# Six more groups whose skip term is turned by DMA, and two transfers moved, in a fused spectral filter and channel MLP on one core

## The chip, the core and the metric

The kernel runs on one core of one Trainium2 chip. The core's engines have queues of their own: TensorE (PE, its weight loads are listed as PEld), VectorE (DVE), ScalarE (ACT), GpSimd (POOL) and SyncE (SP), which here only issues DMAs. DMAs issued by SP and by POOL share 16 DMA engines. The metric is the device time of one execution in microseconds, less is better. Before the change three runs took 514.1, 515.17 and 517.45 us, median 515.17.

## What is computed

The input x has 8 batches of 3136 rows and 256 channels. First each channel is filtered along the rows in the frequency domain, then a low-rank mix along the rows is added, then a two-layer MLP over the channels with its skip:

```python
# x: (8, 3136, 256); filt_r, filt_i: (1569, 256)
X = np.fft.rfft(x, axis=1)
Y = X * (filt_r + 1j * filt_i)[None]
x = np.fft.irfft(Y, n=3136, axis=1)
# U: (3136, 32), V: (32, 3136), w_ch1: (256, 1024), w_ch2: (1024, 256)
xt = x.transpose(0, 2, 1)
u = x + (xt @ U @ V).transpose(0, 2, 1)
return u + np.maximum(u @ w_ch1, 0.0) @ w_ch2
```

## The kernel before

Everything is in float16 with float32 sums in PSUM. 3136 is 49 x 64, and the Fourier transforms are done as matmuls in stages. A batch goes through them in this order.

- Stage 1 (`f1`, L249; for batches 0 and 1 `f1_turned`, L282): four x tiles, loaded by POOL (`load_x`, L127), are multiplied by a 49-point transform. From batch 2 on the result goes to DRAM (`asb` to `ct1` and `ct0`, L256 and L257).
- Stages 2 and 3 (`mid`): from batch 2 on four loads bring the result back in another layout (`a` from `ct`, L327 and L330, called stage 2's loads). Thirteen items follow, each a 64-point transform (`pz`, L385), the filter on DVE (`uv`, L393, L397, L398) and the transform back (`pe`, L344, evicted by ACT at L354). The spectrum goes to DRAM (`ct2`, L363).
- `load_e2` (L417) brings the spectrum back as rows of the tile `eb`, in three parts, called the rows; `rank` adds the 32 low-rank rows.
- Stage 4 (`s4`, L457) multiplies `eb` into `ut`, which is u of one batch with the channels on the partitions.

The MLP runs on 49 groups of 512 rows, counted over all batches. For each group `mm1` (L489, ReLU on ACT at L492) makes eight hidden tiles, and `mm2` (L522) multiplies them by `w2sb`. The last loop of the kernel is the schedule, written out by hand: 392 steps, eight to a group. Step 8n + t issues `mm1(groups[n], t)`, then `mm2(groups[n - 1], t)`, then whatever `plan[8n + t]` holds. The other stages of the next batch are cut into pieces, and `deal` spreads the pieces over the plan. What a step issues on an engine stands in that order in the engine's queue, but the queues run independently of one another: SP and POOL work ahead of PE as far as data and buffers let them.

The output needs u added, and u lies transposed in `ut`. There are two ways. `residual` (L514) multiplies pieces of `ut` by an identity matrix on PE, eight matmuls for a group that lies in one batch, and DVE then copies the sum out of PSUM (L538). For the groups in `turn_at`, `turn_u` (L502) has SP issue two DMA transposes, a pair, that write the turned u into a tile `tur`, and DVE adds it while it evicts (L535). `tur` has three buffers, so each pair waits for the add of the third turned group before it. The first of a group's two evictions comes at t = 3 of its `mm2`, the second at t = 7; then POOL stores the group's output (L542).

For b from 1 to 7 the plan treats a stretch of steps from a = S[b-1] to z = S[b], in which groups of batch b-1 are mixed while batch b goes through its stages. S is 0, 48, 96, 144, 192, 240, 288, 336, 392. e is z - 17 for b = 1, z - 20 for b = 2 to 5 and z - 22 for b = 6 and 7. In a stretch, in the plan of before:

- the rows of batch b are loaded at e - 5, e - 4 and e + 1;
- stage 2's loads of batch b + 1 are issued at e + 2 (z - 12 for b = 1);
- the x loads of batch b + 1 stand at a - 8, a - 6, a - 4 and a - 2 (9, 11, 13, 15 for b = 1);
- for b > 1 three groups, a/8 + 1 to a/8 + 3, are turned at a + 1, a + 2 and a + 3, and the last whole group, z/8 - 1, at z - 9. For b = 1 these are groups 2, 3 and 4 at 15, 16 and 17, and group 5 at 39. From step 337 on groups 43 to 48 are turned in their own steps.

So groups 0, 1, 6, 10, 12, 16, 18, 22, 24, 28, 30, 34, 36, 40 and 42 go through `residual`. Ahead of the loop POOL issues the second batch's x, `w2sb` (L604) and, since nothing holds it, the third batch's first x loads.

Of the kernel before, what the change touches and what calls it, by code (L numbers as in the profile page):

```python
# [14 lines left out]
NB = 8  # L15
# [7 lines left out]
NG = NB * SEQ // GT  # L23
# [56 lines left out]
def kernel(  # L80
# [11 lines left out]
    nc = tc.nc  # L92
# [18 lines left out]
    def bank(tag, name, dtype=F32):  # L111

        return ps.tile([128, 512 if dtype == F32 else 1024], dtype, tag=tag, bufs=4 if tag == "z" else 2, name=name)

    def dram(t, off, dims):
        return bass.AP(tensor=t, offset=off, ap=[list(d) for d in dims])
# [7 lines left out]
    def load_x(b, c):  # L124
        t = sb.tile([98, 8 * DM], F16, tag="x", bufs=4, name="x")
        for a, n in ((0, 96), (96, 2)) if b == 0 else ((0, 98),):
            nc.gpsimd.dma_start(t[a:a + n], dram(x.tensor, (b * SEQ + 8 * c + 32 * a) * DM, [[32 * DM, n], [1, 8 * DM]]))  # L127
        xt[b, c] = t
# [51 lines left out]
    w2sb = cst.tile([128, 8, DM], F16)  # L180
# [16 lines left out]
    seen = cst.tile([128, 4], F16)  # L197
# [42 lines left out]
    def f1(b):  # L240
        for c in range(4):
            t = xt[b, c].rearrange("p (j d) -> p j d", d=DM)
            asb = sb.tile([98, 8, DM], F16, tag="asb", bufs=3, name="asb")
            for half in range(2):
                for i in range(2):
                    pf = bank("z", "pf")
                    for s in range(2):
                        j = 4 * half + 2 * i + s
                        nc.tensor.matmul(pf[0:98, 256 * s:256 * s + 256],  # L249
                                         ws[:, (8 * c + j) * 98:(8 * c + j + 1) * 98], t[:, j, :],  # L250
                                         start=(s == 0), stop=True, skip_group_check=True)
                    dst = asb[:, 4 * half + 2 * i:4 * half + 2 * i + 2, :]
                    src = pf[0:98].rearrange("p (j d) -> p j d", d=DM)
                    nc.scalar.copy(dst, src)  # L254
                    if half and i:
                        nc.sync.dma_start(dram(ct1[b], 8 * c * 96 * DM, [[DM, 96], [96 * DM, 8], [1, DM]]), asb[0:96])  # L256
                        nc.sync.dma_start(dram(ct0[b], 8 * c * DM, [[32 * DM, 2], [1, 8 * DM]]),  # L257
                                          asb[96:98].rearrange("p j d -> p (j d)"))
                    yield
# [8 lines left out]
    def f1_turned(b):  # L268
        t1[b] = (sb.tile([128, 2, 24, 128], F16, tag="ut", bufs=2, name="t1"),
                 sb.tile([128, 2, NR], F16, tag="t10", bufs=1, name="t10"))  # L270
        for c in range(4):
            t = xt[b, c].rearrange("p (j d) -> p j d", d=DM)
            for n in range(4):
                half, dh = n // 2, n % 2
                pf = bank("z" if b else ("z", "m", "z", "o")[n], "pf")
                if b == 0:

                    unread(pf, 2 if (c, n) == (3, 0) else 0)
                    unread(pf, 1, 120)
                for s in range(4):  # L280
                    j = 4 * half + s
                    nc.tensor.matmul(pf[:, 98 * s:98 * s + 98], t[:, j, 128 * dh:128 * dh + 128],  # L282
                                     ws[:, (8 * c + j) * 98:(8 * c + j + 1) * 98],
                                     start=(s == 0), stop=True, skip_group_check=True)
                j = 8 * c + 4 * half

                copy = nc.vector.tensor_copy if dh and not (b and c < 1) else nc.scalar.copy
                copy(t1[b][0][:, dh, :, 4 * j:4 * j + 16].rearrange("p k (j c) -> p k j c", c=4),
                     view(pf, 0, [[1, 24], [98, 4], [24, 4]]))
                copy(view(t1[b][1], NR * dh + j, [[1, 4], [32, 2]]), view(pf, 96, [[98, 4], [1, 2]]))  # L290
                yield
# [201 lines left out]
        gr.h.append(h)  # L493


    turn_at = {}

    def turn_u(gr):
        gr.tu = sb.tile([128, 2, 4, 128], F16, tag="tur", bufs=3, name="tur")
# [5 lines left out]
    def residual(gr, o, i):  # L505
        last = []
        for b, t0, so, n in gr.seg:
            a, z = max(so, 128 * i), min(so + n, 128 * i + 128)
            for dh in range(2):
                if a < z:  # L510
                    p = a - 128 * i
                    last.append((o[p:p + z - a, 128 * dh:128 * dh + 128], utv(b)[:, dh, t0 + a - so:t0 + z - so], dh))
        for d, w, dh in last:
            nc.tensor.matmul(d, w, idn, start=False, stop=(dh == 1), skip_group_check=True)  # L514

    def mm2(gr, t):
        i, half = t // 2, t % 2
        if t % 4 == 0:
            gr.pc = bank("o", "pc")
        o = gr.pc[:, 256 * (i % 2):256 * (i % 2) + 256]  # L520
        for tt in range(4 * half, 4 * half + 4):
            nc.tensor.matmul(o, gr.h[tt][:, 128 * i:128 * i + 128], w2sb[:, tt, :],  # L522
                             start=(tt == 0), stop=(tt == 7 and gr.n in turn_at), skip_group_check=True)
        if half and not gr.n in turn_at:
            residual(gr, o, i)

        parts = {3: (0, 1), 5: (2,), 7: (3,)} if gr.n == NG - 1 else {3: (0, 1), 7: (2, 3)}
        if t not in parts:
            return
        if t == 3:  # L530
            gr.och = sb.tile([128, 4, DM], F32, tag="och", bufs=2, name="och")
        a, n = parts[t][0], len(parts[t])
        dst, src = gr.och[:, a:a + n, :], gr.pc[:, 256 * (a % 2):256 * (a % 2 + n)]
        if gr.n in turn_at:
            nc.vector.tensor_add(dst.rearrange("p g (h d) -> p g h d", h=2), src.rearrange("p (g h d) -> p g h d", h=2, d=128),  # L535
                                 gr.tu[:, :, a:a + n, :].rearrange("p h g d -> p g h d"))
        else:
            nc.vector.tensor_copy(dst, src.rearrange("p (j d) -> p j d", d=DM))  # L538
        if gr.n == NG - 1:
            nc.sync.dma_start(dram(out.tensor, (gr.n * GT + 128 * a) * DM, [[DM, 128], [128 * DM, n], [1, DM]]), dst)  # L540
        elif t == 7:
            nc.gpsimd.dma_start(dram(out.tensor, gr.n * GT * DM, [[DM, 128], [128 * DM, 4], [1, DM]]), gr.och)  # L542


    S = [8 * (b * SEQ // GT) for b in range(NB)] + [8 * NG]
    plan = [[] for _ in range(8 * NG)]

    def deal(gen, count, a, z):
        for i in range(count):
            plan[max(0, int(a + i * (z - a) / count))].append(gen)  # L550

    def later_x(b, c):
        load_x(b, c)
        yield

    f1s = [f1(b) if b > 1 else f1_turned(b) for b in range(NB)]
    mids = [mid(0, "o")] + [mid(b) for b in range(1, NB)]
# [2 lines left out]
    turns = [turn_u(gr) for gr in groups]  # L560
# [38 lines left out]
    for h in range(2):  # L599
        for p in (32, 64):  # L600
            nc.gpsimd.tensor_copy(seen[p:p + 32], eb[p:p + 32, 8 + 32 * h, 0:4])  # L601
        for c in ((1,), (2, 3))[h]:
            load_x(1, c)
    nc.gpsimd.dma_start(w2sb, moe_w_ch2.rearrange("(t cc) e -> cc t e", t=8))  # L604
    for _ in s4s[0]:
        pass

    def loads(b, part):
        load_e2(b, part)
        yield  # L610

    for b in range(1, NB):
        a, z = S[b - 1], S[b]
        e = z - (17 if b == 1 else 20 if b < 6 else 22)
        deal(mids[b], 13, a + {1: 8, 2: -3}.get(b, -5), e - 4)
        deal(mids[b], 4, e - 4, e)
        for p, at in enumerate((e - 5, e - 4, e + 1)):
            plan[at].append(loads(b, p))
        deal(ranks[b], 6, e, e + 6)
        if b + 1 < NB:  # L620

            plan[z - 12 if b == 1 else e + 2].append(mids[b + 1])

        n = a // 8 + (1 if b > 1 else 2)
        turn_at.update({n + i: a + (1 if b > 1 else 15) + i for i in range(3)})
        turn_at[z // 8 - 1] = z - 9
        deal(s4s[b], 16, e + 8, z - 2)
        if b == 1:
            deal(f1s[1], 12, 1, 8)
        if b + 1 < NB:  # L630

            for c in range(4):
                plan[a + (9 if b == 1 else -8) + 2 * c].append(later_x(b + 1, c))
            deal(f1s[b + 1], 16, a + (21 if b == 1 else 10), z - (13 if b == 1 else 20))

    turn_at.update({n: 8 * n + 2 for n in range(S[NB - 1] // 8 + 1, NG)})
    for n, at in turn_at.items():
        plan[at].append(turns[n])
    for n, gr in enumerate(groups):
        for t in range(8):  # L640
            mm1(gr, t)
            if n:
                mm2(groups[n - 1], t)
            for gen in plan[8 * n + t]:
                next(gen, None)
# [32 lines left out]
```

## Time and profile before

| what | value |
|---|---|
| profiled execution, device time | 515.22 us |
| its span, first to last instruction | 513.4 us |
| mean granted TensorE clock | 0.988 |
| ACT, ReLU of `mm1` (L492) | 392 x 604 ns |
| PE, `mm2` (L522) | 1568, 234.3 us busy |
| PE, `mm1` (L489) | 896, 234.0 us busy |
| PE, identity matmuls (L514) | 128, 8 of them for pieces at a border of batches |
| DVE, add and evict (L535) / copy (L538) | 69 / 30 |
| SP, DMA transposes (L502) | 68, 1.19 to 8.83 us each to issue, median 1.33 |
| POOL, x loads of 392 KB | 28, median 10.7 us to landing |
| DMA queues, share of 16 engines | SP's 44.3%, POOL's 30.8% |

The profile is one execution; its time around the span is 1.8 us. Busy PE is modelled and matmuls overlap, so the price of a matmul is read from the distance between two starts. For DMAs issued by SP the profile tells the time of issue but not of landing; a landing shows only where something waits for it. "Idle before" in brackets names what ended an engine's idle time.

### The profile page before, as it was taken

What the parts mean: (1) busy time and instruction counts of PE and PEld (TensorE: products, weight loads), DVE (VectorE), ACT (ScalarE), POOL (GpSimd) and SP (SyncE); (2) the same over time, 40 slices, a digit from 0 to 9 for tenths busy, and PEclk for the clock granted to TensorE, in tenths of its full rate; (3) what the DMA queues carried; (4) which work ended last, traced back from release to release, by engine and by line L of the source; (5) the groups of instructions that cost most, each with busy time, mean ns of one, the idle gap of its engine ahead of it and who ended that gap; (6) DMA issues with size and microseconds to landing.
All of it is one profiled execution on the core that took longest, in us unless ns stands there. A gap on an engine that the chain in (4) does not pass through costs nothing.

```text
span 513.4 us, 11535 instructions
## 1 busy us (share of the span) xinstructions
PE 483.8 (94%) x4580; PEld 340.7 (66%) x4580; DVE 350.9 (68%) x470; ACT 375.7 (73%) x704; POOL 80.6 (16%) x122
## 2 busy tenths in 40 slices
PE   4886799996899999999999999999999999999996
PEld 4545466774576777677667777677667766776665
DVE  5886499584875797479867898479847896731122
ACT  6873678964697679866897689867996677666663
POOL 6662010020010210030010200120001010101110
PEclk9997999999899999999999999999999999999999
DMA  8987929999458996799568994899688456343243
GB/s 194 167 202 176 176 53 210 291 249 185 123 171 269 260 182 206 232 263 210 166 183 279 243 198 149 254 265 186 214 256 237 126 125 226 104 124 104 72 113 124
DMA packets 104383, 97.13 MB, mean 189 GB/s; under 512 B 41843, under 2 KB 88883, under 8 KB 104328
## 3 DMA queue, kind: packets, MB, share of 16 engines
q1 hardware_dynamic: 89624, 54.80, 44.3%
q0 software_dynamic: 14704, 41.58, 30.8%
q8 instruction: 36, 0.59, 0.4%
q14 instruction: 19, 0.16, 0.1%
HBM read 55.20 MB, written 47.78 MB: 201 GB/s over the span
## 4 chain that ended last, share of the span: by engine, by line
PE 78%; DMA 9%; DVE 6%; ACT 2%; SPq 1%; issue 1%; POOL 0%; POOLq 0%; DVEq 0%; ACTq 0%
PE pc L522 30%; PE phh L489 29%; PE pu L457 4%; PE pf L249 4%; PE pe L344 4%; DVE uv L393 3%; PE pz L385 3%; DMA tur<-ut 3%; DMA w2sb<-in_moe_w_ch_dram 2%; DMA ct<-e 2%; DMA eb<-ct 1%; PE pc L514 1%; PE ph L424 1%; ACT e L354 1%; DVE uv L398 1%; DVE uv L397 1%
## 5 line engine op out<-in xcount | busy, mean ns | idle before, releaser
L492 ACT ACTIVATE h<-phh 128x512 f16<-128x512 f32 x392 | 235.8, 604 | 81.4 <-PE phh L489 80.4
L522 PE MATMUL pc<-w2sb,h 128*128 128x256 f16 x1568 | 234.3, 273 | 2.6 <-DMA w2sb<-in_moe_w_ch_dram 2.0
L489 PE MATMUL phh<-ut,w1sb 128*128 128x512 f16 (+7 forms) x896 | 234.0, 353 | 0.4 <-DVE ut L464 0.4
L522 PEld LDWEIGHTS <-h 128*128 128x128 f16 x1568 | 151.9, 98 | 94.0 <-issue 3.8
L393 DVE TENSOR_TENSOR uv<-pz,fab 128x1024 f16<-128x1024 f32 (+1 forms) x104 | 120.6, 1177 | 10.7 <-PE pz L385 9.0
L542 POOL DMA_DIRECT2D out_dram<-och x48 | 38.8, 809 | 399.7 <-DVE och L535 256.8
L535 DVE TENSOR_TENSOR och<-pc,tur 128x512 f32<-128x512 f32 (+1 forms) x69 | 47.0, 682 | 78.6 <-PE pc L522 71.2
L489 PEld LDWEIGHTS <-w1sb 128*128 128x128 f16 x896 | 80.0, 98 | 26.5 <-issue 7.7
L354 ACT CAST e<-pe 128x512 f16<-128x512 f32 x96 | 56.5, 590 | 22.1 <-PE pe L344 21.0
L464 DVE CAST ut<-pu 128x392 f16<-128x392 f32 x92 | 48.8, 559 | 20.8 <-PE pu L457 17.4
L254 ACT CAST asb<-pf 98x512 f16<-98x512 f32 x96 | 57.2, 598 | 0.1
L344 PE MATMUL pe<-uv,m 128*128 128x512 f16 (+1 forms) x117 | 41.5, 373 | 7.9 <-DVE uv L398 5.6
L439 DVE COPY eb<-h 32x4096 f16<-32x4096 f16 x32 | 38.2, 1231 | 13.8 <-ACT h L436 13.8
L457 PE MATMUL pu<-sv,eb 97*128 97x49 f16 x1024 | 41.4, 188 | 4.6 <-DMA eb<-ct 4.6
L457 PEld LDWEIGHTS <-eb 97*128 97x128 f16 x1024 | 39.0, 99 | 6.7 <-issue 5.1
L385 PE MATMUL pz<-a,m 128*128 128x512 f16 x96 | 36.2, 379 | 1.1 <-DVE a L310 1.0
L249 PE MATMUL pf<-x,ws 98*98 98x256 f16 x192 | 36.6, 273 | 0.1
L538 DVE COPY och<-pc 128x512 f32<-128x512 f32 x30 | 20.7, 691 | 19.4 <-PE pc L514 19.0
L397 DVE TENSOR_TENSOR uv<-uv 64x1024 f16<-64x1024 f16 (+1 forms) x49 | 30.8, 629 | 1.7
L398 DVE TENSOR_TENSOR uv<-uv 64x1024 f16<-64x1024 f16 (+1 forms) x49 | 30.7, 627 | 0.7
L249 PEld LDWEIGHTS <-ws 98*98 98x98 f16 x192 | 22.7, 125 | 9.5 <-issue 0.8
L462 ACT CAST ut<-pu 128x392 f16<-128x392 f32 x36 | 17.5, 485 | 10.8 <-POOL seen L601 6.1
(79 smaller groups left out, 237.2 us busy)
## 6 DMA issues: line engine op xcount, KB each, us to landing
out_dram<-och POOLq DMA_DIRECT2D x48, 512.0 KB, 4.9
ct<-e SPq DMA_DIRECT2D x47, 256.0 KB
eb<-ct SPq DMA_DIRECT2D x46, 256.0 KB
x<-in_x_dram POOLq DMA_DIRECT2D x28, 392.0 KB, 10.7
ct<-asb SPq DMA_DIRECT2D x24, 384.0 KB
a<-ct SPq DMA_DIRECT2D x18, 512.0 KB
x<-in_x_dram POOLq DMA_DIRECT2D x4, 384.0 KB, 7.9
tur<-ut SPq DMA_TRANSPOSE x68
```

What stands on the lines that cost most here:

```text
L249: nc.tensor.matmul(pf[0:98, 256 * s:256 * s + 256], ws[:, (8 * c + j) * 98:(8 * c + j + 1) * 98], t[:, j, :], start=(s == 0), stop=True, s ...
L254: nc.scalar.copy(dst, src)
L344: nc.tensor.matmul(pe[:, 0:n], w, uv[:, f, o:o + n], start=(f == 0), stop=(b > 0 or f == 1))
L354: nc.scalar.copy(t[:, 2 * (i % 2):2 * (i % 2) + 2, :].rearrange("p k d -> p (k d)"), pe)
L385: nc.tensor.matmul(pz, a2m, src[:, k:k + 2, :].rearrange("p k d -> p (k d)"), start=True, stop=True)
L393: nc.vector.tensor_mul(uv[:, :, o:o + n], zin, fin)
L457: nc.tensor.matmul(pu[:, NQ * i:NQ * i + NQ], eb[:, 8 * n + i, d], sv[:, 8 * g + i, :], start=(i == 0), stop=True, skip_group_check=True)
L464: nc.vector.tensor_copy(dst, src)
L489: nc.tensor.matmul(ph[:, o:o + n], w1sb[:, dh, 128 * t:128 * t + 128], utv(b)[:, dh, t0:t0 + n], start=(dh == 0), stop=(dh == 1), skip_gro ...
L492: nc.scalar.activation(h, ph, RELU)
L522: nc.tensor.matmul(o, gr.h[tt][:, 128 * i:128 * i + 128], w2sb[:, tt, :], start=(tt == 0), stop=(tt == 7 and gr.n in turn_at), skip_group_ ...
L535: nc.vector.tensor_add(dst.rearrange("p g (h d) -> p g h d", h=2), src.rearrange("p (g h d) -> p g h d", h=2, d=128), gr.tu[:, :, a:a + n, ...
```

## The change

Pairs are now put into the plan where the stretch is dealt, by a small function, and not in a loop at the end; `turning` is the set of turned groups. The plan differs in four things. In each stretch from b = 2 to 6 a fifth group, z/8 - 2 (10, 16, 22, 28, 34), is turned at e + 1, behind the last part of the rows; for the last stretch it is group 40 at step 322. The third pair of a stretch goes from a + 3 to a + 8. Group 5's pair goes from step 39 to step 33, which puts it behind the rows of step 32 and ahead of the last stage 1 store and of stage 2's loads. And POOL copies four columns of `w2sb` into a spare tile right after issuing its load, so that POOL waits for w2's landing before it goes on to the third batch's x.

```diff
-    turn_at = {}
+    turning = set()
...
+    def turn_at(at, n):
+        turning.add(n)
+        plan[at].append(turns[n])
...
     nc.gpsimd.dma_start(w2sb, moe_w_ch2.rearrange("(t cc) e -> cc t e", t=8))
+
+    nc.gpsimd.tensor_copy(seen, w2sb[:, 7, 0:4])
...
         for p, at in enumerate((e - 5, e - 4, e + 1)):
             plan[at].append(loads(b, p))
         deal(ranks[b], 6, e, e + 6)
+        if 1 < b < NB - 1:
+
+            turn_at(e + 1, z // 8 - 2)
...
         n = a // 8 + (1 if b > 1 else 2)
-        turn_at.update({n + i: a + (1 if b > 1 else 15) + i for i in range(3)})
-        turn_at[z // 8 - 1] = z - 9
+        for i in range(3):
+            turn_at(a + (15 + i if b == 1 else (1, 2, 8)[i]), n + i)
+        turn_at(z - (15 if b == 1 else 9), z // 8 - 1)
...
-    turn_at.update({n: 8 * n + 2 for n in range(S[NB - 1] // 8 + 1, NG)})
-    for n, at in turn_at.items():
-        plan[at].append(turns[n])
+    turn_at(S[NB - 1] - 14, S[NB - 1] // 8 - 2)
+    for n in range(S[NB - 1] // 8 + 1, NG):
+        turn_at(8 * n + 2, n)
```

In `mm2`, `gr.n in turn_at` becomes `gr.n in turning`; nothing else there changes.

## The prediction

> **What bounds the kernel now.** I read the page first (busy shares and the 40 slices), then the waits, then the timeline around the one dark slice of PE, then the DMA windows around the transposes.
>
> ```profile
> PE 483.8 (94%) x4580; PEld 340.7 (66%) x4580; DVE 350.9 (68%) x470; ACT 375.7 (73%) x704; POOL 80.6 (16%) x122
> ...
> PE   4886799996899999999999999999999999999996
> ```
>
> Each digit is 12.8 us. From slice 5 on PE is full but for slice 9 (115 to 128 us). So work taken off PE counts in full, and idle time of PE has to be looked for in two places only. The waits (us in total, times, longest) name them:
>
> ```profile
> DVE och L535 <- DMA tur<-ut: 6.3, 1, 6.3
> ...
> PE pe L344 <- DVE uv L398: 5.6, 1, 5.6
> ...
> PE pc L522 <- DMA w2sb<-in_moe_w_ch_dram: 2.0, 1, 2.0
> ```
>
> The first two are one event. The timeline of SP's queue shows its start, that of PE its end (start, duration, line, shapes, idle time before):
>
> ```profile
> 105.99 0.34 SPq L330 DMA_DIRECT2D a<-ct  x1
> ...
> 108.16 26.47 SPq L502 DMA_TRANSPOSE tur<-ut  x8
> 134.68 0.58 SPq L363 DMA_DIRECT2D ct<-e  x1
> ```
>
> ```profile
> 123.99 0.38 PE L385 MATMUL pz<-a,m 128*128 128x512 f16 x1
> 129.99 0.59 PE L344 MATMUL pe<-uv,m 128*128 128x512 f16 x1 [5.62 <-DVE uv L398]
> 130.37 1.06 PE L489 MATMUL phh<-ut,w1sb 128*128 128x512 f16 x2
> 131.23 1.06 PE L522 MATMUL pc<-w2sb,h 128*128 128x256 f16 x4
> 132.08 0.86 PE L489 MATMUL phh<-ut,w1sb 128*128 128x512 f16 x2
> 132.78 0.60 PE L522 MATMUL pc<-w2sb,h 128*128 128x256 f16 x4
> ```
>
> Group 5's pair of transposes is issued at 108.2 and 110.4, behind the four a loads, and lands at 126.6 by the chain of waits (110.44 plus 16.14). DVE's add (L535) waits, its later uv work waits behind it, and PE stands still. After that the starts are 0.86 apart where two L489 matmuls take 0.43: the granted clock in 129 to 134 is 0.66. Why 16 us? The DMA view of two windows, first 117 to 123, while the four x loads issued at 107.2 to 109.3 run, then 128 to 130 without them:
>
> ```profile
> DMA packets 573, 1.03 MB, mean 171 GB/s; under 512 B 341, under 2 KB 341, under 8 KB 573
> ```
>
> ```profile
> DMA packets 1006, 0.24 MB, mean 120 GB/s; under 512 B 1006, under 2 KB 1006, under 8 KB 1006
> ```
>
> A transpose moves 128 KB in packets of about 240 bytes, so over 500 of them. Beside x loads 57 a microsecond get through, alone about 500. A pair caught in an x load lasts until that load ends.
>
> **Group 5's pair, from step 39 to step 33.** (A step is one turn of the last loop, 1.1 to 1.3 us.) SP now issues it right behind the row loads of 99.80 to 100.96, at about 101 to 104, and the x loads come at 107.2 as before. It should land near 106, and the add wants it at 120.4: 14 us to spare. Its buffer is that of group 2, whose second add comes before the output store issued at 97.5. Gain: from 123.99 to 129.99 there are 6.00 us where L385 to the next start takes 0.21 (119.64 to 119.85): 5.8. The slow clock: from 129.99 to 132.78 PE does 1.51 us of work (0.22 + 0.43 + 0.43 + 0.43) in 2.79, and 0.1 more is lost behind it: 1.4. What comes next: at 120.4 DVE had nothing else late, and before the stall PE was full, so PE's own pace is next. Cost: each issue takes SP 1.3 us (median of L502), so 2.6 for the last ct store of stage 1 (101.69) and then the a loads, which wait for that store's landing. The first a load, issued at 105.99, moves to about 108.6, and PE wants it at 113.76 (L385). An SP load's landing isn't shown; the nearest row, Pool's 512 KB output store, has 4.9, which gives 113.5. Ends 0 and 1 us, and I take 0, since nothing waited there with 7.8 us.
>
> **Six more groups turned (10, 16, 22, 28, 34, 40).** Each loses 8 matmuls and 8 weight loads of L514. On PE a pair of them costs the distance to the next start:
>
> ```profile
> 171.85 0.28 PE L514 MATMUL pc<-idn,ut 128*128 128x128 f16 x2
> 171.96 0.58 PE L457 MATMUL pu<-sv,eb 97*128 97x49 f16 x16
> ```
>
> 0.11 us for two, 48 in all: 2.7 us, all of it on the path, as PE has no gaps in those slices. Twelve evictions change from L538 (691 ns) to L535 (689 ns): nothing. The pair's own landing is safe: in the stretch of groups 6 to 11 the row loads go out at 162.40, the new pair would follow at about 163.7, and the first eviction of group 10 comes near 175.
>
> The cost is what stands behind it on SP: the a loads and then the stretch's last pair (groups 11, 17, 23, 29), 2.7 us later by issue time and about 1 us more by the packets. The a loads have room: issued at 163.66, wanted at 174.85 (L385). The last pair has less than it seems. Group 11's 1,000 small packets all pass in 171 to 175, the x loads (issued from 171.41) fill 176 to 185, and the add comes at 185.20. So 2 to 4 us later its second transpose falls into the x loads, as group 5's does now. How late it can be is bounded by the end of the x loads. The last of each four lands at 185.9, 241.7, 298.3 and 356.9 (issue plus the longest landing), the first adds that need the pair are at 185.20, 241.32, 297.56 and 353.68, and each will be 0.45 earlier, as PE is. Late by 1.2, 0.8, 1.2 and 3.7: 6.9 us at most, 0 if the pair slips through ahead. Groups 35 and 41 have no x loads beside them. I take 2: half of the bound, less some 0.4 of cover each (DVE's 6.29 became 5.8 on PE), where DVE is nearly full (8.8 of 9 us in 349 to 358).
>
> **Third pair of each stretch from step a+3 to a+8.** On SP it now lets spectrum stores (L363) pass; it has room: group 15's, issued from 190.6 on, is used at 221.9. Nothing either way. Pair 9 moves in the same way, to step 56.
>
> **Third batch's x behind w2.** Pool gets one copy of 4 columns (0.18 us by L601) that waits until w2 lands (61.7). Behind it on Pool stand three x loads (now 50.45, 54.54 and 57.12) and group 0's store (75.34). They would go out at 62 to 64 and, at 6.6 to 12.9 us to landing, be there by 77; stage 1 wants the first at 82.5, so no cost. The gain is PE's 2.05 us wait at 59.7, or nothing. Counting packets of 512 B to 2 KB, w2 has 522 in 53 to 57, 438 in 57 to 59 and 62 in 59 to 62: x packets flow only as w2 runs out, as if each engine had finished w2 before it took up the next load. Then those x packets don't delay the last 62. I take 0, end 2.05.
>
> The Trainium skill ("DMA: Bandwidth & Descriptors", "Queues, rings and completion order") says that within one queue each DMA engine takes descriptors in ring order. By that rule x, issued behind w2 on the same queue, is behind it already, and this part is worth 0; if it did not hold, the sum would be 2.05 lower.
>
> **Sum.** On the profiled execution's own 515.2 us (span 513.4, 1.8 around it; the median of the runs, 515.17, is the same): 515.2 - 5.8 - 1.4 - 2.7 = 505.3, plus 2 for the last pairs: 507.3.
>
> **Rivals.**
> *w2 gains* (0.13): the three x loads do share with w2. For it: x landed 1.6 us behind w2 (50.45 + 12.9). 505.3 - 2.05 = 503.2, up to 505.3 with a part of it.
> *Last pairs wait out the x loads in full* (0.13): 509 to 512.2 (505.3 + 6.9). For it: group 29's margin is the worst by 2.5 us. Against: the store before the x loads leaves 2 us of free passage.
> The same section of the skill says that an engine takes turns between queues packet by packet. That speaks for this rival, and 57 small packets a microsecond beside x packets agrees.
> *Group 5's pair still lands late* (0.07), for instance because SP is held ahead of it: 515.2 - 2.7 = 512.5.
> *Slower* (0.07): the last pair's first transpose falls into the x loads too, so that the second starts only when they are over. Then four stretches each get group 5's stall, 7.2 us with the clock: 505.3 + 29 = 534. It turns the gain into a loss from 2.5 us a stretch and into over 1% from 3.8 (15.1 / 4). Against it: three of the four adds come within 0.9 us of the end of the x loads already.
>
> **Chances.** A run of this kernel can tell about 1%, 5.2 us. The forecast, 505.3 to 509, has 0.60. Faster by over 1% (below 510.0): 0.60 + 0.13 + 0.04 of the second rival = 0.77. Within: 0.09 + 0.07 = 0.16. Slower 0.07. Range 503.3 to 512.2: from w2's gain to the full bound; what lies outside is the late pair, the slower case and a bit of w2's end, under 0.2.
>
> **What would show it.** Group 5: no wait of L535 on tur, granted clock 1.0 in the whole of 115 to 135. Residuals: L514 down from 128 to 80. Last pairs: new waits L535 on tur near groups 11, 17, 23, 29, the one of 29 the longest, each followed by a PE gap a little shorter. w2: the wait of L522 stays near 2. I am wrong if PE shows gaps over 3 us, or if the a loads (L385) become a wait at the start of a batch.

## The result and the profile after

The change made the kernel slower.

| kernel | runs | median us | lowest to highest | ratio to before, 95% interval |
|---|---|---|---|---|
| before | 6 | 514.63 | 510.83 to 517.45 | |
| after | 6 | 530.58 | 529.79 to 542.35 | 1.032 [1.026, 1.038] |

The forecast was 507.3 us with a range up to 512.2, so 18 us lie outside the range. The profiled execution of the changed kernel is its longest one, 542.35 us (span 540.6, mean granted clock 0.972). The other five lie between 529.8 and 534.0. Here and below the ratios leave out executions more than 1.5% longer than the fastest of their kernel, while the medians keep them. All sums below are made against 542.35, and what they show is larger there than in the median.

The page's busy row and slices of PE, each digit now 13.5 us:

```profile
PE 486.9 (90%) x4532; PEld 338.5 (63%) x4532; DVE 349.3 (65%) x470; ACT 375.7 (69%) x704; POOL 80.6 (15%) x123
...
PE   4886999969999799993999929999699999999997
```

48 matmuls fewer on PE, as forecast, and the dark slice of group 5 (115 to 128 us) is gone. In its place stand slices 13, 18, 23 and 28 (counted from 0), one stretch of the schedule apart, and slice 8 (108 to 122 us) is darker than its neighbours. The waits (us in total, times, longest):

```profile
DVE och L535 <- DMA tur<-ut: 35.8, 4, 12.4
...
PE pc L522 <- DVE och L535: 22.3, 4, 9.7
...
PE pe L344 <- DVE uv L393: 6.1, 4, 4.8
PE pz L385 <- DMA a<-ct: 4.7, 1, 4.7
```

The add of a turned group waits for its pair four times, and 22.3 + 4.8 us of that reach PE (4.8 is the longest wait of L344, behind the last of the four adds; its other three are as short as before). A fifth wait, 4.7 us, is that of stage 2 for its first a load. The chain of waits says whose pairs they are (start, us, what):

```profile
165.65 19.82 DMA tur<-ut
...
228.74 24.00 DMA tur<-ut
...
293.85 26.31 DMA tur<-ut
...
361.45 19.92 DMA tur<-ut
```

These are the second transposes of groups 11, 17, 23 and 29, the last pairs of four stretches. They take 20 to 26 us, where group 5's took 16 before the change. None of the added pairs (10, 16, 22, 28) is waited for.

How one of these stalls comes about is seen around group 17. First SP's queue, then POOL's:

```profile
220.53 3.60 SPq L502 DMA_TRANSPOSE tur<-ut  x2
224.23 0.51 SPq L330 DMA_DIRECT2D a<-ct  x1
...
227.50 24.95 SPq L502 DMA_TRANSPOSE tur<-ut  x6
```

```profile
227.41 0.75 POOL L542 DMA_DIRECT2D out_dram<-och  x1 [6.86 <-DVE och L535]
228.16 2.18 POOL L127 DMA_DIRECT2D x<-in_x_dram  x4
```

The new pair (group 16) holds SP for 3.6 us, then come the a loads, and group 17's pair is issued at 227.50 and 228.74: the first transpose 0.1 us behind POOL's store at 227.41, the second behind the first x load at 228.16. Before the change that pair stood at 222.78 and 224.13, the store at 226.80: its second transpose was 2.7 us ahead of the store, and is now 1.3 us behind it. Then DVE and PE at the add:

```profile
252.94 0.69 DVE L535 TENSOR_TENSOR och<-pc,tur 128x512 f32<-128x512 f32 x1 [11.38 <-DMA tur<-ut]
```

```profile
244.40 0.60 PE L489 MATMUL phh<-ut,w1sb 128*128 128x512 f16 x2
253.68 1.01 PE L522 MATMUL pc<-w2sb,h 128*128 128x256 f16 x4 [8.69 <-DVE och L535]
```

DVE stands still for 11.4 us and PE for 8.7 of these. The x loads end late as well. Their four landings are 246.7, 249.7, 252.1 and 252.6. From first issue to last landing that is 24.4 us, and 14.1 for the same loads before the change. The page's medians of the big x loads (KB each, us to landing) say the same, first before, then after:

```profile
x<-in_x_dram POOLq DMA_DIRECT2D x28, 392.0 KB, 10.7
```

```profile
x<-in_x_dram POOLq DMA_DIRECT2D x28, 392.0 KB, 16.5
```

The DMA view of 234 to 241 in the changed kernel (busy share in tenths, then the sum), and under it the nearest window of before, 232 to 241, also within the x loads of batch 5:

```profile
DMA  9923819959595953554627253535962595959499
...
DMA packets 466, 0.57 MB, mean 81 GB/s; under 512 B 347, under 2 KB 347, under 8 KB 465
```

```profile
DMA packets 1072, 1.62 MB, mean 180 GB/s; under 512 B 720, under 2 KB 720, under 8 KB 1071
```

While the pair and the x loads meet, the DMA engines move less than half of what they did, and the busy row dips more often. Of the 118 packets of 4 KB that start in this window, all of POOL's queue, half take 0.32 us or less, as before, but 17 take 1.3 to 5.5 us (before 0 of 351 took over 1 us). Counting the 256-byte packets (those of the transposes, some 510 each) by the microsecond in which they start shows the pair's own way:

```
group 17, before: 227: 317  228: 180  229: 514  230: 13  (the pair is through)
group 17, after:  232: 55  233: 247  234: 115  235: 30  236: 24  237: 20  238: 23
                  239: 23  240: 26  241: 38  242: 44  243: 56  244: 105  245: 127
```

Before the change the whole pair passes in three microseconds, in the time that the store takes. After it, some 400 packets pass, then 20 to 30 a microsecond. At that rate the first transpose, half of the packets, needs until about 239 (an estimate), so it too falls into the x loads.

**Where the time went.** The forecast's certain terms give 505.3. PE's new waits add 22.3 + 4.8 + 4.7 less 0.5 that before had too, 31.3: 536.6. The rest, 5.7, is what remains, and the slow clock behind the waits fits it: L489 and L522, the same matmuls as before, are 7.9 us longer busy, while PE's wait for w2 is 1.5 shorter. The clock behind two of the waits (us, PE busy, granted clock, DMA share, GB/s, for 14 and 15 us at groups 17 and 23):

```profile
244.00:258.00 14.00, 5.31 (x27) 0.76 1.16 162
310.00:325.00 15.00, 5.34 (x27) 0.67 1.12 159
```

A clock of 0.76 and 0.67 loses up to 3.4 and 5.0 us, of which a part lies in the stall itself. The Trainium skill ("TensorE: Matmul & The Clock Gate", "Part 1: The HAM clock gate") puts the point from which PE drops to half rate at about 3.4 us of idleness. Here each of the five gaps, 3.4 to 9.7 us, has a stretch of half clock at its end or behind it, so the trace agrees.

### The profile page after: what moved, and what is told of

It reads as the page before. It is cut to its first block, busy times and chain, and to the rows that moved or that the text cites. A ratio compares the mean times of both kernels' runs of the same rounds, so it can differ in the third digit from the quotient of the medians.

```text
span 540.6 us, 11465 instructions
## 1 busy us (share of the span) xinstructions
PE 486.9 (90%) x4532; PEld 338.5 (63%) x4532; DVE 349.3 (65%) x470; ACT 375.7 (69%) x704; POOL 80.6 (15%) x123
## 4 chain that ended last, share of the span: by engine, by line
PE 60%; DMA 27%; DVE 6%; ACT 3%; issue 1%; POOL 1%; SPq 1%; DVEq 0%; ACTq 0%; POOLq 0%
PE pc L522 24%; PE phh L489 23%; DMA tur<-ut 17%; PE pf L249 3%; PE pe L344 3%; DVE uv L393 3%; PE pu L457 2%; PE pz L385 2%; DMA x<-in_x_dram 2%; DMA w2sb<-in_moe_w_ch_dram 2%; DMA a<-ct 2%; DMA ct<-e 2%; DMA ct<-asb 2%; DVE och L535 1%; DMA eb<-ct 1%
## 5 line engine op out<-in xcount | busy, mean ns | idle before, releaser
L522 PE MATMUL pc<-w2sb,h 128*128 128x256 f16 x1568 | 238.6, 276 | 22.8 <-DVE och L535 22.3
L489 PE MATMUL phh<-ut,w1sb 128*128 128x512 f16 (+7 forms) x896 | 237.6, 357 | 0.5 <-DVE ut L464 0.5
L522 PEld LDWEIGHTS <-h 128*128 128x128 f16 x1568 | 153.7, 99 | 118.2 <-issue 29.1
L535 DVE TENSOR_TENSOR och<-pc,tur 128x512 f32<-128x512 f32 (+1 forms) x81 | 55.3, 683 | 116.8 <-PE pc L522 79.7
L393 DVE TENSOR_TENSOR uv<-pz,fab 128x1024 f16<-128x1024 f32 (+1 forms) x104 | 120.3, 1177 | 14.2 <-PE pz L385 12.8
L489 PEld LDWEIGHTS <-w1sb 128*128 128x128 f16 x896 | 80.6, 98 | 27.0 <-issue 8.4
L464 DVE CAST ut<-pu 128x392 f16<-128x392 f32 x92 | 48.3, 558 | 17.1 <-PE pu L457 15.2
L344 PE MATMUL pe<-uv,m 128*128 128x512 f16 (+1 forms) x117 | 42.3, 379 | 7.1 <-DVE uv L393 6.1
L439 DVE COPY eb<-h 32x4096 f16<-32x4096 f16 x32 | 38.2, 1231 | 13.8 <-ACT h L436 13.8
L457 PE MATMUL pu<-sv,eb 97*128 97x49 f16 x1024 | 39.2, 185 | 3.5 <-DMA eb<-ct 3.5
L385 PE MATMUL pz<-a,m 128*128 128x512 f16 x96 | 36.6, 383 | 5.8 <-DMA a<-ct 4.7
L457 PEld LDWEIGHTS <-eb 97*128 97x128 f16 x1024 | 37.7, 96 | 5.6 <-issue 3.5
L538 DVE COPY och<-pc 128x512 f32<-128x512 f32 x18 | 12.4, 689 | 11.7 <-PE pc L514 11.5
## 6 DMA issues: line engine op xcount, KB each, us to landing
x<-in_x_dram POOLq DMA_DIRECT2D x28, 392.0 KB, 16.5
```

Source lines behind the costliest of these rows:

```text
L344: nc.tensor.matmul(pe[:, 0:n], w, uv[:, f, o:o + n], start=(f == 0), stop=(b > 0 or f == 1))
L385: nc.tensor.matmul(pz, a2m, src[:, k:k + 2, :].rearrange("p k d -> p (k d)"), start=True, stop=True)
L393: nc.vector.tensor_mul(uv[:, :, o:o + n], zin, fin)
L457: nc.tensor.matmul(pu[:, NQ * i:NQ * i + NQ], eb[:, 8 * n + i, d], sv[:, 8 * g + i, :], start=(i == 0), stop=True, skip_group_check=True)
L464: nc.vector.tensor_copy(dst, src)
L489: nc.tensor.matmul(ph[:, o:o + n], w1sb[:, dh, 128 * t:128 * t + 128], utv(b)[:, dh, t0:t0 + n], start=(dh == 0), stop=(dh == 1), skip_gro ...
```

## The experiments

The theory after the result: the new pair pushes the last pair back by what SP needs to issue it. The last pair then meets the x loads, both slow down, and the add comes too late. Rivals: the other two edits are to blame (group 5's move, the w2 hold), or the third pair's step, or the added bytes and not the transposes. The kernels were run beside fresh runs of before on the same chip, so each has a ratio of its own.

### The changed kernel once more

> The changed kernel once more, for a second profile. Theory A (the fifth pair pushes each stretch's last pair into the x loads, and transposes and x loads slow each other): about 530 us, L535 waiting on tur for groups 11, 17, 23 and 29, 20 to 36 us in all, PE standing still for 3 to 10 us after each, and the granted clock at 0.5 behind each. Theory B (the moved transfers, group 5's pair and w2's hold, cost the time): about 530 us too, but with the idle time of PE before 125 us.

526.15 us median (516.48 to 533.81, 4 runs), ratio 1.010 [1.004, 1.016] from the two shortest, 1.023 by the medians (before 514.44 beside it). The profiled execution, 516.48 us, is the shortest one and has only two of the four stalls:

```profile
DVE och L535 <- DMA tur<-ut: 13.2, 2, 8.7
```

They are groups 11 and 17. The pair now runs a race with POOL's store and x loads, and the two profiles differ in how many of the four stretches lose it. By both measurements it is slower. The x loads of batches 4 to 7 take 19.2, 25.5, 20.0 and 19.3 us here.

### One part alone

Group 5's pair alone, on the kernel before:

```diff
-        turn_at[z // 8 - 1] = z - 9
+        turn_at[z // 8 - 1] = z - (15 if b == 1 else 9)
```

> Only group 5's pair at step 33 instead of 39. Theory A: 511 to 517 us; L535's wait on tur at group 5 is gone (-7.2), but L385 waits near 5 us for the first a load (as at 108.8 in the changed kernel's profile), with the slow clock -5 + 7 in sum. No wait on tur elsewhere. Theory B: 520 us or more.

510.77 us (505.55 to 513.24, 10 runs), ratio 0.990 [0.987, 0.994]. No wait on tur is left. But a new one takes most of its place:

```profile
PE pz L385 <- DMA a<-ct: 4.5, 1, 4.5
```

So this edit is a gain of 1%, 3.7 us by the medians, smaller than the forecast's 7.2 by about the wait for the a load.

The w2 hold alone, on the kernel before:

```diff
+    nc.gpsimd.tensor_copy(seen, w2sb[:, 7, 0:4])
```

> Only the hold of the third batch's x behind w2. If each DMA engine takes one queue's transfers in order, the wait of L522 on w2 stays near 2 us and the time at 514 to 515. If x shared with w2, as the 0.5 us wait in the changed kernel's profile hints: the wait is 0.5 us and the time 1 to 2 us less, 513. Theory B: over 515.

516.49 us (512.12 to 517.62, 12 runs), ratio 1.003 [1.000, 1.005]. PE's wait for w2 was 0.9 us in place of 2.0, and the time didn't fall (group 5's stall was 8.1 us in that profile, 2.5 longer than in that of before). Without the hold that wait was 2.0 in the profile of before, 1.9 in that of the next experiment and 0.4 in that of group 5's pair alone, so it also varies by itself. No gain, as forecast.

The six added groups and the third pairs' step alone, on the kernel before (the diff of the change without the group 5 and w2 lines):

> Only the fifth pairs (groups 10, 16, 22, 28, 34, 40) and the third pair of a stretch at a + 8; group 5's pair at 39 and x not held. Theory A: 522 to 538 us, the four waits on tur of the changed kernel and in addition that of group 5. Theory B: 512.5 us, 2.7 less than before.

533.21 us (522.0 to 543.2, 4 runs), ratio 1.022 [1.015, 1.028] from the two shortest, 1.036 by the medians, with the waits of the changed kernel beside group 5's old one:

```profile
DVE och L535 <- DMA tur<-ut: 36.4, 5, 12.0
```

The loss is in this part.

The changed kernel without the six groups, the third pairs' step kept:

```diff
-        if 1 < b < NB - 1:
-            turn_at(e + 1, z // 8 - 2)
...
-    turn_at(S[NB - 1] - 14, S[NB - 1] // 8 - 2)
```

> The changed kernel without the fifth groups: group 5's pair at 33, the third pair at a + 8, x held behind w2. Theory A (the fifth pairs push the last pairs into the x loads): like the run with group 5's pair alone, 509 to 513 us, no wait of L535 on tur, x loads of batches 4 to 7 landing 8 to 15 us after issue. Theory C (the third pair's new step lets other transfers by and delays the last pair): waits on tur stay, 520 us or more.

511.52 us (505.06 to 514.98, 10 runs), ratio 0.993 [0.989, 0.998]. No wait on tur at all, x loads of 13.7 to 15.4 us. So without the added pairs the loss is gone, and the third pairs' step alone makes none.

### Taking pair and x loads apart

The x loads of batches 4 to 7 later in the plan, in the changed kernel:

```diff
-                plan[a + (9 if b == 1 else -8) + 2 * c].append(later_x(b + 1, c))
+                plan[a + (9 if b == 1 else -8 if b == 2 else -2) + 2 * c].append(later_x(b + 1, c))
```

> The changed kernel with the x loads of batches 4 to 7 six steps later in the plan (a - 2 instead of a - 8); all twelve new transposes stay. Theory A: no wait on tur at groups 11, 17, 23 and 29, PE without gaps there, 506 to 510 us with the first a load's wait of 1.5 to 5 us still there. Theory D (twelve more transposes cost by their number, wherever the x loads are): 520 us or more.

511.83 us (502.59 to 520.41, 10 runs). The ratio, 0.983 [0.977, 0.988], rests on the three shortest; by the medians it is 0.994, and the median missed the expected 506 to 510. In POOL's queue the first x load still follows the same store; the other three now stand behind the next one, some 11 us later. Waits on tur: 1.7 us in two; the wait for the first a load is 6.2 us here. With three quarters of the x bytes out of the way the same pairs, issued at the same places, come in time.

The reverse, in the kernel before: the x loads at a - 14, where they go out together with the a loads and ahead of the last pair, so that all of them meet:

```diff
-                plan[a + (9 if b == 1 else -8) + 2 * c].append(later_x(b + 1, c))
+                plan[a + (9 if b == 1 else -8 if b == 2 else -14) + 2 * c].append(later_x(b + 1, c))
```

> The kernel before, nothing turned in addition, with the x loads of batches 4 to 7 six steps earlier (a - 14 instead of a - 8), so that they meet the last pairs of groups 11, 17, 23 and 29. Theory A: the collision is enough by itself; new waits on tur, x loads landing up to 16 us or more after issue, 520 us or more. Theory D: 514 us as before, perhaps less, since the first x data comes earlier.

517.55 us (514.14 to 525.52, 10 runs), ratio 1.003 [1.000, 1.007]. The 520 us and more that the theory asked for were missed:

```profile
DVE och L535 <- DMA tur<-ut: 16.7, 5, 8.5
```

The longest, 8.5, is group 5's; the other four are 0.9, 2.0, 1.8 and 3.5 us. The second transposes of these last pairs landed 17.7 to 20.0 us after their issue, against 20 to 26 in the changed kernel, although there is only one pair here. The x loads took 22.4 to 24.5 us, but a part of that is their issue: the fourth now stands behind the next store, some 8 us after the first. They began 8 to 9 us earlier than before, so the adds waited little. A pair that meets the x loads lands late, and what it costs is set by how far the add is from there.

The last pair ahead of stage 2's loads, in the changed kernel:

```diff
             turn_at(e + 1, z // 8 - 2)
+            turn_at(e + 1, z // 8 - 1)
...
-        turn_at(z - (15 if b == 1 else 9), z // 8 - 1)
+        if b in (1, NB - 1):
+            turn_at(z - (15 if b == 1 else 9), z // 8 - 1)
```

> The changed kernel with the last pairs (11, 17, 23, 29, 35) issued right behind the fifth ones, ahead of stage 2's loads; x loads where they were. Theory A: the last pairs land before the x loads, no wait on tur, 506 to 512 us; the a loads are now the ones beside the x loads, and L385 may wait for them, up to 2 us a stretch. Theory D: 520 us or more.

508.65 us (505.67 to 509.05, 4 runs), ratio 0.985 [0.978, 0.992]. All the added groups are turned and there is no wait on tur. The last pair's second transpose is issued 1.1 to 2.6 us ahead of the store. The a loads, now at the store and the first x loads, stretch the x loads to 17.2 to 18.8 us. Against the kernel without the six groups (511.52) the median is 2.9 us less; the forecast had 2.7 for their matmuls, but the ranges of the two kernels overlap.

### Transposes or bytes

In the changed kernel, the last pairs (11, 17, 23, 29, 35) or the fifth pairs (10, 16, 22, 28, 34) become plain copies of the same bytes that nothing reads. These five groups then go through `residual`, so the output stays whole.

```diff
+    def copy_u(gr):
+        tu = sb.tile([128, 2, 4, 128], F16, tag="tur", bufs=3, name="tur")
+        for b, t0, o, n in gr.seg:
+            for dh in range(2):
+                nc.sync.dma_start(tu[:, dh, :, :].rearrange("p g d -> p (g d)"), utv(b)[:, dh, t0:t0 + n])
+        yield
+
-    def turn_at(at, n):
+    def turn_at(at, n, plain=False):
+        if plain:
+            plan[at].append(copy_u(groups[n]))
+            return
...
-            turn_at(e + 1, z // 8 - 2)
+            turn_at(e + 1, z // 8 - 2, True)   # fifth pairs plain
...
-        turn_at(z - (15 if b == 1 else 9), z // 8 - 1)
+        turn_at(z - (15 if b == 1 else 9), z // 8 - 1, 1 < b < NB - 1)   # last pairs plain
```

Each kernel has one of the two last edits.

> After, but the last pairs of the stretches (groups 11, 17, 23, 29 and 35) are plain copies of the same bytes into a tur buffer that nothing reads, issued at the same step; their groups take the skip term from PE (5 x 8 matmuls of L514, 2.2 us). Theory T (it is the transposes that hold up the x loads): the x loads of batches 4 to 7 go from first issue to last landing in 14 to 16 us as before the change (19 to 25 in the changed kernel), no wait of L535 on tur, 509 to 513 us. Rival Q (any load that follows on SP and meets the x loads does it, by its bytes and its place): the x loads still take 18 us and more; L535 has no wait, but waits of PE behind the x loads or the a loads may stay, 511 to 518 us.

Last pairs plain: 509.65 us (505.33 to 510.38, 4 runs), ratio 0.989 [0.984, 0.995]. No wait on tur; x loads of 14.3, 14.2, 16.3 and 16.8 us. Plain copies at the same step are issued in 0.5 to 1.0 us each and are out of the way; they don't stretch the x loads. The last a load is issued 1.9 to 2.7 us ahead of the store here, nearly as late as in the changed kernel (0.4 to 2.1), so it is the transposes that the 19 to 25 us need, and not bytes or a loads that come this late.

> After, but the fifth pairs (groups 10, 16, 22, 28 and 34) are plain copies of the same bytes at the same step, read by nothing; their groups take the skip term from PE (2.2 us more). Theory T: the last pair is still transposed and still comes later than before the change by what SP takes to issue the copies and by their bytes; it meets the x loads, which take over 18 us, L535 waits for tur in two to four groups by 4 to 12 us each, 516 to 535 us. Rival R (two pairs of transposes in one stretch are needed, plain copies let the last pair through): no wait of L535 over 2 us, x loads 14 to 16 us, 511 to 514 us.

Fifth pairs plain: 512.97 us (504.09 to 517.82, 4 runs; before 514.4 beside it, 0.997 by the medians). One wait is left, after x loads of 14.4, 14.2, 14.7 and 20.6 us:

```profile
DVE och L535 <- DMA tur<-ut: 1.6, 1, 1.6
```

Neither of the two expectations fits whole. The issue times say why (us from the issue of the last pair's second transpose to that of POOL's store in front of the x loads, negative where the transpose is later; x loads from first issue to last landing, batches 4 to 7):

| kernel | transpose ahead of the store | x loads |
|---|---|---|
| before | 2.7, 2.7, 2.2, 3.0 | 14.5, 14.1, 14.5, 17.0 |
| after | -0.3, -1.3, -0.1, -0.1 | 23.4, 24.4, 24.5, 19.5 |
| after, second measurement | -0.7, -0.3, 0.0, 0.5 | 19.2, 25.5, 20.0, 19.3 |
| six groups and third pairs' step alone | -0.5, -0.5, -0.6, -0.2 | 16.8, 23.8, 19.4, 25.5 |
| fifth pairs plain | 2.2, 1.4, 1.8, 1.3 | 14.4, 14.2, 14.7, 20.6 |

Plain copies hold SP for less, so the last pair keeps 1.3 to 2.2 us ahead of the store. In these five kernels it gets through from 1.4 us on, and at 1.3 and below it does not; with the a loads behind the pair 1.1 was enough. So what decides is the place of the last pair, not that there are two pairs: with both pairs ahead of the a loads nothing waits, and with the x loads earlier a single pair lands as late. In the second measurement the pairs with 0.0 and 0.5 met the x loads too, and their adds still came in time.

### The transfers by themselves

Two kernels run only transfers and compute nothing of the reference. The first puts pairs beside four x loads:

> Transfers by themselves, none of the reference's computation: four x loads alone, a pair of transposes alone, both released together (one pair, then two), plain copies of the same bytes instead of two pairs, and two pairs released when the first x load has landed; three times each. Theory A (transposes and x loads slow each other beyond sharing): four x loads alone take 9 to 10 us from first issue to last landing, a pair alone 4, together over 14, and the plain copies with x loads under 13. Theory D (plain sharing): together no more than the sum of both, with transposes as with plain copies.

Four x loads took 11.5 us alone, 12.5 with one pair and 14.8 with two (first round, from first issue to last landing). In all three rounds of the phase with two pairs the first of the transposes landed with the last x load (53.7 against 53.5, 127.6 against 127.9, 202.2 against 202.4). Neighbouring phases overlapped, so these times show no loss beyond sharing and can't rule one out. The second kernel has the a loads and the store too:

> Transfers by themselves, nothing of the reference is computed: three a loads on SP, behind them nothing, a pair of transposes, plain copies of the same bytes, a pair on both sides of the a loads, or a pair ahead of the last a load; beside them POOL's store and four x loads, begun one or two POOL copies (about 3 us each) later. Theory T: the four x loads take 16 us and more with a pair that meets them and at most 14 with nothing or with plain copies, and the window in which they meet shows under 100 GB/s. Rival Q: pair and plain copies give the same within 1.5 us. Rival S (everything only shares, as in the first measurement by itself): 11.5 us with nothing, 12 to 14 with anything beside them.

| on SP | x loads, three rounds, us | second transpose of the last pair, issue to landing |
|---|---|---|
| a loads | 14.5, 13.8, 14.5 | |
| a loads, pair; store 0.1 to 0.3 us ahead of its second transpose | 14.4, 15.4, 15.2 | 14.3, 14.7, 15.0 |
| the same, store and x later | 13.2, 14.1, 12.9 | 5.7, 6.2, 5.5 |
| a loads, plain copies, store 0.6 to 0.9 us behind them | 14.1, 14.7, 14.9 | |
| pair, a loads, pair; store and x with the a loads | 16.8, 17.3, 17.2 | 14.4, 14.9, 14.8 |
| pair, a loads; store and x with the a loads | 16.5, 16.7, 16.3 | |

Shown by itself: a transpose that meets the x loads lands with them, 14 to 15 us after its issue, and 5.5 to 6.2 us where it is 1.3 to 1.7 us ahead of the store (third row). In the fifth row both transposes of the second pair land with the last x load (121.9 and 122.3, x at 121.7). The a loads stretch the x loads by 2.3 us on the mean (16.5 against 14.2). The pair of the second row adds 0.7, to 15.0, where the theory asked for 16 and more. In the changed kernel the last a load is issued 0.4 to 2.1 us ahead of the store, in the kernel before 4.6 to 5.2, so the a loads may have a part in its 19 to 25 us. The 14.2 to 16.8 us with plain last pairs, whose a loads are nearly as late, and the 17.2 to 18.8 with the last pairs ahead, whose a loads are later still, say how small a part. Why the transposes stretch the x loads so much further there, and why the engines fall to 81 GB/s, these kernels don't reproduce: it stays open.

### The wait for the a load, and the best kernel

With the last pairs ahead, 5.7 us of waits of L385 on the a loads are left. Two edits on top of that kernel: group 5's pair two steps earlier, or the third batch's x six steps later.

```diff
-            turn_at(z - (15 if b == 1 else 9), z // 8 - 1)
+            turn_at(z - (17 if b == 1 else 9), z // 8 - 1)
```

> Both pairs at the end of a stretch ahead of stage 2's loads, as in the run before, and group 5's pair two steps earlier (31), ahead of the last rows instead of behind them. Theory S (the first a load comes late because SP issues the pair just ahead of the last stage 1 store): the wait of L385 near 110 us falls from 4 to under 1 us, and 504 to 506 us. Theory X (it comes late because the third x loads' four transfers, issued 1 to 2 us ahead of it, now go first): the wait stays at 3 to 6 us, 508 us.

```diff
-                plan[a + (9 if b == 1 else -8) + 2 * c].append(later_x(b + 1, c))
+                plan[a + (9 if b == 1 else -2 if b == 2 else -8) + 2 * c].append(later_x(b + 1, c))
```

> Group 5's pair at 33, but the x loads of batch 3 six steps later. Theory S: the wait of L385 near 110 us stays at 3 to 6 us, 508 us. Theory X: it falls under 1 us, 504 to 506 us.

> Both of the two edits. Either theory: no wait of L385 over 1 us, 503 to 506 us; all terms of the prediction without the prices that it had too small (515 - 7.2 - 2.7 = 505).

| kernel | median us (lowest to highest) | ratio to before | L385 on a |
|---|---|---|---|
| pair earlier | 506.55 (504.08 to 510.45) | 0.984 [0.979, 0.989] | 2.1 |
| x later | 504.25 (503.11 to 508.81) | 0.981 [0.975, 0.985] | none |
| both | 504.13 (502.45 to 509.7) | 0.980 [0.975, 0.985] | 1.2 |

With x later one x load of batch 3 goes out with the a loads and three 10 us behind it; the first a load, issued at 105.3, is there when PE wants it at 111.9. So the x loads of batch 3 held the a load up. The order on SP has a part too: the earlier pair alone, with the a load still 1.0 us behind the first x load, took 3.6 of the 5.7 us off, where one theory expected under 1 us left and the other 3 to 6. The last two kernels beat the kernel before by 2%, with all the added groups turned. The profile of the one with x later has no dark slice behind the start:

```profile
PE   3887799999999999999999999999999999999997
```

## Why the prediction was wrong

- **Group 5's pair.** Right. It is issued at 96.1 and 97.6, its add has no wait, and the granted clock is 1.00 from 120 to 136.
- **The a loads behind it, 0 us with an end of 1.** Too small: 4.5 us with this edit alone, 4.7 in the changed kernel, 1.4 in its second measurement. The forecast took the landing of POOL's store, 4.9 us, as the nearest row. The first a load took 9.4 us, from 104.30 to PE's start at 113.7. In the profile of before the x loads of batch 3 were issued 1.2 us behind it. With the pair ahead of it on SP, it is issued about 2 us behind the first x load (104.30 and 102.22). That x load wasn't in the forecast's term; with three of the four moved away the wait is gone.
- **The six groups' matmuls, 2.7.** Nothing speaks against it: PE has 48 matmuls fewer, and 2.9 us lie between the medians of the kernels with and without the six groups (508.65 and 511.52) where neither has a wait on tur. Their ranges overlap, and their waits for the a loads differ.
- **w2, 0.** Right within what can be measured: 1.003 [1.000, 1.005]. The wait is 0.4 to 1.5 us in the profiles with the hold and 0.4 to 2.0 in those without it.
- **The third pairs' step, 0.** Right: no wait on tur in the kernel that has it without the six groups.
- **The last pairs, +2 with a bound of 6.9.** This step failed. The delay was forecast about right, 2.7 us by issue time and 1 more by the packets, where 2.3 to 4.0 us were measured against the store, and so was its first result: "its second transpose falls into the x loads". Then the forecast bounded the lateness by "the end of the x loads", 185.9 to 356.9 us as they stood in the profile of before. Two things of this were false. The x loads don't end where they ended: with a pair among them their 14 to 17 us become 19 to 25. And the first transpose fell into them as well, as the packets of group 17's pair show. Nor did the margins to that end order the waits: group 29's was to be the longest and was 6.0 us, those of groups 17 and 23 were 11.4 and 12.4. PE lost 26.6 us here (22.3 + 4.8, less 0.5) and most of the 5.7 put down to the clock.
- **The rival on the slower side** had this mechanism, "the last pair's first transpose falls into the x loads too", and 534 us against 530.58 measured. It was given 0.07, because "three of the four adds come within 0.9 us of the end of the x loads already". That reason took the same fixed end for granted. The row that spoke for it was in sight: the forecast counts "2 us of free passage" between pair and x loads, and the change takes 2.7 by the forecast's own count, of the 2.2 to 3.0 that there were. That 534 lies so near 530.58 is in part luck: the rival priced each of the four stretches at 7.2 us, the waits of PE were 3.4, 8.7, 9.7 and 4.8, and executions run from 516.5 to 542.4.

The floor of 505.3 that the certain terms gave was real: 504.25 and 504.13 us, once the last pairs and the a load are out of the x loads' way.

## What to carry to other kernels

The end of another transfer is a bound for a delay only if that transfer stays as it is; where the delayed one joins it, both ends move. Before a DMA is put in front of others on a queue, look at what the last of them has to be ahead of on the other queues, and by how much: here 2.2 to 3.0 us of lead, and 2.3 to 4.0 us taken. A small transfer with a due time belongs ahead of the large loads, its own queue's and the others'.

## What the runs showed that was not expected

The changed kernel, measured twice, gave medians of 530.6 and 526.2 us, and single executions from 516.5 to 542.4, while before stayed within 510.2 and 520.9 over all its runs. A schedule that is won or lost by a microsecond in four places would spread its times like this; the second profile, with two of the four waits, fits that. While a pair of transposes and the x loads met, the DMA engines moved 81 GB/s, where the same loads ran at 180 without it. By themselves such transfers moved 184 GB/s (50 to 54 us of the second transfer kernel). The Trainium skill ("DMA: Bandwidth & Descriptors", "Queues, rings and completion order") has each engine take turns between queues packet by packet. The 20 to 30 small packets a microsecond, beside 12 to 20 larger ones in 235 to 239, are in keeping with that; the packets that took up to 5.5 us are not explained by it, and no run here tells what held them.
